# A gated mix of a long convolution and a product-key expert layer on one core: frequency products in whole-array form, folded keys in one burst, skip transforms in pairs, the last tile by halves

## The chip, the cores and the metric

The kernel runs on one core of a Trainium2 chip. The metric is the device time of one execution in microseconds (us), as the median of several runs. The engines are called by their names in the profile: PE is TensorE's matmul, PEld its weight load, DVE is VectorE, ACT is ScalarE, POOL is GpSimd, SP is SyncE, whose queue issues the DMAs.

## What is computed

Two branches read the same 2048 tokens of width 576, and a gate per token mixes them.

```python
g = sigmoid((x * gate_w).sum(-1))
# a: state-space convolution, by FFT of length 4096
K = einsum("dn,dnl,dn->dl", Cc, exp(dt*A*l), dB).real
a = irfft(rfft(pad(u)) * rfft(pad(K)))[:L] + u * Dskip
# b: product-key experts, 32 heads, 64 x 64 keys, 2 experts a head
q = x @ w_q;  s1 = q[:128] @ k1.T;  s2 = q[128:] @ k2.T
top 2 of s1, top 2 of s2, top 2 of their sums -> experts, softmax
b = sum(softmax * gelu(x . u[expert]) * v[expert])
out = g * a + (1 - g) * b
```

## The kernel before

A Python body writes out the whole program in one pass. It keeps a model clock for TensorE (`clock`) and for the other engines (the class `Engine`, lines 108 to 125), and a heap of generators. The main loop issues matmuls of the dense work; after every few of them `pump()` (line 206) lets the generators whose model time has come write their instructions. So the order on every queue is fixed when the program is built, and the chip runs each queue in that order, waiting on semaphores. All matmuls go through `mm` (line 197), hence nearly all rows of the profile have line 204, and all other computing goes through line 124: the tile names tell the work apart.

The dense work is of three kinds. `s` (line 1488) is a score group, one of 128: 14 fp16 matmuls of 512 columns, tokens against the keys that were folded into w_q; its 512 scores a token go through MAX8 and FIND_INDEX8 on DVE (`scores_top`, line 813). `a` (line 1506) is an activation group, one of 128: 14 such matmuls, tokens against the expert table u; ACT or DVE scales the result (`go`) and it is stored to `g_d`. `o` (line 1538) is the output, 16 tiles of 192 fp16 matmuls of 288 columns: 32 weight blocks `wh`, three products each, for two column halves in turn. All `s` and `a` groups come before the first `o`. The last 26 `a` groups are kept for the time after the last `s` group (line 1481).

Beside the dense work run these generators.

- **Folded keys** (`w_half`, lines 465 to 508, and `w_tail`): for each of 8 chunks and 2 halves, w_q times the keys as fp32 matmuls of 64 columns into a 64-column part of the array (tile `wb`), in three bursts of 32, 32 and 16 instructions on the chip; between bursts the generator yields for 2 us, so other matmuls come between. Each burst takes one PSUM bank and one of two `hw` tokens.
- **Convolution kernel** (`k_front`, `k_gen`: tiles `kP`, `kb`; 36 chunks) and the first transforms (`u1_`, `k1_`), with their PSUM banks of the same four as the folded keys in this part of the program.
- **Frequency products** (`products`, lines 1015 to 1105). The 64-point second stage of the transforms, the product and the inverse second stage, in 16 rows by 3 column parts, 48 blocks. A block has 4 fp32 matmuls for the signal (`pu`) and 4 for the kernel (`pk`), each 192 columns into a 64-column part of the array, then a tail on ACT (`us`, `ks`: one copy each from PSUM), two products and two half-size sums on POOL (or DVE), and 4 fp32 matmuls of 192 columns with 64 rows for the inverse (`pv`), issued three blocks later. After the products, the pools of the next stage are opened, `prep(0)` begins, and the last five chunks of the expert table v are split (`v_work(3, 5)`, `v_work(5, 8)`, lines 1136 to 1149).
- **Expert weights** (`prep`, line 1300): one-hot tiles `A`, `Be`, `Bg` on DVE, 128 matmuls `S` a tile in four rounds, products on DVE into `gl`, then the split into `wh`. `o` of a tile needs its `wh`.
- **Skip transform** (`y_part`, lines 1363 to 1399): per tile one load of three tensors, 4 fp32 matmuls (`y`, a 64-column part of the array), two sums on DVE, a scaling on ACT. `finish` (line 1403) adds the output of `o` and stores four row blocks.

The lines of a block's matmuls before (f2 and fi are constants, `half` is the lower or upper 64 partitions):

```python
for r in range(2):
    for z in range(2):
        mm(pb[half[z], PW * r:PW * r + PW], f2[:, 64 * r:64 * r + 64], x[:, z, cs], True, True, 0.17)
...
for r in range(2):
    for z in range(2):
        mm(pv[z][:, :PW], fi[r][half[z]], v[half[z], r], r == 0, r == 1, 0.17)
```

The functions that the diff touches:

Of the kernel before, what the change touches and what calls it, by code (L numbers as in the profile page):

```python
# [24 lines left out]
D = 576  # L25
# [13 lines left out]
FM = 576  # L39
KT = FM + 128  # L40
# [3 lines left out]
def _tables():  # L44
# [43 lines left out]
    cst[:, 256:384] = np.tile(fi[0].reshape(64, 128), (2, 1))  # L88
    cst[:, FM:FM + 128] = np.tile(fi[1].reshape(64, 128), (2, 1))
# [39 lines left out]
def body(ctx: ExitStack, tc: tile.TileContext, xT, au, par, logdt, dskip, gatew, wq, kT, uT, vv,  # L129
# [60 lines left out]
    def dma(o, i):  # L190
# [4 lines left out]
        DQ.dma_start(o, i)  # L195
# [82 lines left out]
    quota(sc=4, wb=0, kb=4, hw=2, slot=9, go=3, m8=2, raw=1, ko=2)  # L278
# [33 lines left out]
    ident, f2, fi = cst[:, 0:128], cst[:, 128:256], (cst[:, 256:384], cst[:, FM:FM + 128])  # L312
# [152 lines left out]
    def w_half(c, h, w):  # L465
        fl = lambda x: x.rearrange("p a b -> p (a b)")
        yield from ready(w)
        acc = newcol(True)
        junk = wj.tile([128, 4, D], BF16, tag="wj", name=f"wj{c}_{h}")
        S.activation(fl(junk), fl(w), AF.Square, accum_out=sc[:, acc])  # L470
        yield from ready(junk)
        while not sk:
            yield 0.3
        tag = side()
        yield from need(tag)
        p = bank(tag, f"wn{c}_{h}")
        mm(p[:, 0:1], onesf, sc[:, acc], True, True, 0.1)
        yield from ready(p)
        s, i = root_scale(p[:, 0:1], kk, True)
        V.tensor_copy(invW[:, 2 * c + h:2 * c + h + 1], i)  # L480
        free(tag, s)
        while c not in halves:
            yield 0.3
        hl, rem, count = halves[c]
        o = slice(256 * h, 256 * h + 256)
        for k in (0, 2, 4):
            yield from need("hw")
            tag = side()
# [12 lines left out]
            yield 2  # L501
        free("slot")
        if c > 0:
            free("raw")
        if h == 0 and c > 0:
            spawn(w_next(c, 1))
        elif h == 1 and c < 7:
            spawn(w_next(c + 1, 0))

    def w_tail(c, k, pb, hl, rem, o, count, s, tag):  # L510
        yield from ready(pb, s)
        if k < 4:
            yield from split(hl[:, 0, k:k + 2, o], hl[:, 1, k:k + 2, o], pb.rearrange("p (k n) -> p k n", k=2), s)
            free(tag, hl)
            free("hw", hl)
# [499 lines left out]
    def products(ff):  # L1015
# [11 lines left out]
        half = [slice(0, 64), slice(64, 128)]  # L1027
        made = []

        def tail(nm, pu, pk, v, vo):  # L1030
            two = lambda x: x[:, 0:2 * PW].rearrange("p (r q) -> p r q", r=2)
            t = lambda g, n: ff.tile([128, 2, PW], F32, tag=g, name=g + nm, bufs=n)
            us, ks, t2 = t("us", 2), t("ks", 2), t("t2", 2)
            bc = lambda r: ks[:, r:r + 1].to_broadcast([128, 2, PW])
# [12 lines left out]
            made.append(nm)  # L1047

        def store(k, hh, vo, pv):
            yield from ready(*pv)  # L1050
            copy2([(vo[:, z, PW * hh:PW * hh + PW], pv[z][:, :PW]) for z in range(2)])
            free("wb", vo)
# [15 lines left out]
        for k in range(16):  # L1068
# [7 lines left out]
            for hh in range(3):  # L1076
# [6 lines left out]
                yield from need("wb", 4 if last else 2)  # L1083
# [12 lines left out]
                spawn(tail(nm, *both, v, vo))  # L1096
                del pb, both
        for last in queue:
# [3 lines left out]
            yield from need("wb", 2)  # L1102
# [260 lines left out]
    def y_part():  # L1363
        def load(t):
            a = oy.tile([128, D], F32, tag="ya", name=f"ya{t}", bufs=3)
            au_load(a, t)
            z = oy.tile([128, 2, D], F32, tag="yz", name=f"yz{t}")
# [6 lines left out]
        nxt = load(0)  # L1374
        for t in range(NT):
            a, z, tf = nxt
            yield from ready(a, z, tf, late=4.0)
            G.tensor_mul(a, a, db)
            while t >= 2 and t - 2 not in finished:
                yield 0.5  # L1380
            yield from need("wb", 2)
            pbs = []
            for hh in range(2):
                pb = bank("wb", f"y{t}_{hh}")
                for pr in range(2):
                    mm(pb[64 * pr:64 * pr + 64, :288], tf[:, pr, :], z[:, pr, 288 * hh:288 * hh + 288], True, True, 0.27)
                pbs.append(pb)
            if t + 1 < NT:
                nxt = load(t + 1)
            yield from ready(a, *pbs)  # L1390
            for hh in range(2):
                ah = a.rearrange("p (j b q) -> p b j q", j=2, b=2)[:, hh]
                V.scalar_tensor_tensor(ah, pbs[hh][:, :288].rearrange("p (j q) -> p j q", j=2), iuk, ah,
                                       op0=OP.mult, op1=OP.add)
                free("wb", a)
            del pbs, pb
            yield from ready(a)
            S.activation(a, a, AF.Copy, scale=gA[:, t:t + 1])
            yt[t] = a

    finished = {}

    def finish(t, po):
# [4 lines left out]
        for hh in range(2):  # L1408
            cs = slice(288 * hh, 288 * hh + 288)
            V.scalar_tensor_tensor(a[:, cs], po[hh][:, :288], om[:, t:t + 1], a[:, cs], op0=OP.mult, op1=OP.add)  # L1410
            free("sc", a)
# [113 lines left out]
    for t in range(NT):  # L1525
# [5 lines left out]
        for b in range(32):  # L1531
            if t == 0 and b % 4 == 0:
                until(lambda: len(vhl) > b // 4)
                wait(ready(vhl[b // 4]))
            vt = vhl[b // 4]
# [4 lines left out]
            pump()  # L1540
        free("slot")
# [44 lines left out]
```

## Time and profile before

| what | value |
|---|---|
| median of 3 runs | 1543.64 us (1543.47 to 1545.33) |
| the profiled execution's own time | 1541.05 us |
| its span | 1539.3 us |
| granted TensorE clock, mean of the span | 0.999 |
| PE busy | 1508.4 us, 98% of the span |
| DVE busy | 1211.6 us, 79% |
| ACT busy | 781.1 us, 51% |
| POOL busy | 543.3 us, 35% |

The profiled execution took 2.6 us less than the median. On the chip every fp32 matmul of the program is two weight loads and two matmul instructions; fp16 matmuls have one of each. A row of the timeline merges consecutive instructions of one kind, so the difference between the starts of two rows is what the first of them cost on its engine. The duration of one matmul contains the way through the array, which the next one overlaps.

### The profile page before, as it was taken

The numbers are of one execution on the slowest core, as the hardware profiler recorded it, in microseconds if no ns is written. First come the engines' busy times: TensorE is split into PE (matmuls) and PEld (weight loads), VectorE is DVE, ScalarE is ACT, GpSimd is POOL, SyncE is SP. The second block draws the span as 40 slices with busy tenths as digits, with TensorE's granted clock in tenths as the row PEclk, the third lists the DMA queues.
The fourth block names the chain that finished last, engine by engine and source line by source line (L and its number), as shares of the span: only waits on it lengthen the run. The fifth ranks groups of instructions, "written<-read, shape, count | busy, mean of one in ns | idle before, by whom it ended". The sixth has DMA issues, their size and how long they took to land.

```text
span 1539.3 us, 37510 instructions
## 1 busy us (share of the span) xinstructions
PE 1508.4 (98%) x14278; PEld 919.0 (60%) x14278; DVE 1211.6 (79%) x4589; ACT 781.1 (51%) x1262; POOL 543.3 (35%) x581
## 2 busy tenths in 40 slices
PE   6999999999999999999999999999999999999998
PEld 4445454445554455656555554445778888788786
DVE  7988998998799957786554579968888788888860
ACT  6548976787859742554444434374432332332320
POOL 0454667646554520136767852240100000000000
PEclk9999999999999999999999999999999999999999
DMA  7344553434444459784755634263553343343310
GB/s 263 91 119 140 162 159 94 138 109 147 139 127 127 128 143 229 243 285 143 231 196 167 208 103 150 90 223 124 152 171 127 104 132 115 115 132 107 122 35 16
DMA packets 153844, 223.41 MB, mean 145 GB/s; under 512 B 11840, under 2 KB 105664, under 8 KB 147008
## 3 DMA queue, kind: packets, MB, share of 16 engines
q1 hardware_dynamic: 153664, 221.02, 46.3%
q8 instruction: 112, 1.84, 0.5%
q14 instruction: 68, 0.56, 0.1%
HBM read 149.67 MB, written 71.30 MB: 144 GB/s over the span
## 4 chain that ended last, share of the span: by engine, by line
PE 84%; DVE 9%; DMA 3%; ACT 2%; issue 1%; SPq 0%; DVEq 0%; ACTq 0%
PE o L204 24%; PE s L204 21%; PE a L204 20%; PE S L204 4%; PE wb L204 3%; PE pv L204 3%; PE pu L204 2%; PE pk L204 2%; DVE i L124 2%; PE kb L204 2%; DVE CS L124 1%; PE y L204 1%; DVE uh L124 1%; DVE m L124 1%; DMA sk_d<-k1o 1%
## 5 line engine op out<-in xcount | busy, mean ns | idle before, releaser
L204 PE MATMUL o<-vhl,wh 128*128 128x288 f16 x3072 | 388.2, 286 | 0.0
L204 PE MATMUL s<-whl,xb 128*128 128x512 f16 x1536 | 367.6, 379 | 1.7 <-DVE xb L124 0.7
L204 PE MATMUL a<-xb,uhl 128*128 128x512 f16 x1536 | 364.5, 379 | 0.0
L204 PEld LDWEIGHTS <-wh 128*128 128x128 f16 x3072 | 295.5, 98 | 79.5 <-issue 7.0
L204 PEld LDWEIGHTS <-xb 128*128 128x128 f16 x1792 | 168.6, 98 | 200.6 <-issue 12.5
L204 PEld LDWEIGHTS <-uhl 128*128 128x128 f16 x1536 | 147.7, 98 | 167.4 <-issue 0.5
L124 DVE FIND_INDEX8 i<-m,s 128x8 uint32<-128x64 f32 x1024 | 206.3, 221 | 0.0
L124 DVE MAX8 m<-s 128x8 f32<-128x64 f32 x1024 | 146.3, 214 | 51.6 <-PE s L204 51.0
L124 ACT ACTIVATE wh<-gl,s_wg 128x1024 f16<-128x1024 f32 x64 | 68.8, 1137 | 179.3 <-DVE gl L124 179.3
L124 POOL TENSOR_TENSOR ya<-ya,db 128x576 f32<-128x576 f32 x16 | 24.7, 1542 | 355.3 <-DMA ya<-in_au_dram 115.7
L124 POOL TENSOR_TENSOR CS<-CS,ex 128x512 f32<-128x512 f32 x72 | 97.8, 1391 | 146.5 <-DVE ex L124 134.8
L124 DVE TENSOR_TENSOR gl<-S,gl 128x256 f32<-128x256 f32 x256 | 90.4, 415 | 20.7 <-PE S L204 18.6
L124 ACT ACTIVATE go<-a,i_a 128x512 f32<-128x512 f32 x86 | 58.8, 686 | 76.7 <-PE a L204 59.7
L124 DVE SCALAR_TENSOR_TENSOR wh<-gl,s_wg,wh 128x1024 f16<-128x1024 f32 x63 | 84.7, 1368 | 13.2 <-ACT wh L124 13.2
L124 ACT ACTIVATE gl<-gl 128x1024 f32<-128x1024 f32 x64 | 63.7, 1046 | 52.6 <-DMA gl<-g_d 52.6
L124 POOL TENSOR_TENSOR e<-aN,rt 128x512 f32<-128x512 f32 x72 | 81.5, 1152 | 25.0 <-PE kb L204 25.0
L124 DVE TENSOR_TENSOR Bg<-Be,vals 128x1024 f16<-128x1024 f16 x128 | 83.9, 696 | 2.2
L124 DVE TENSOR_TENSOR A<-iota_a,vals 128x2048 f16<-128x2048 f16 x64 | 79.3, 1240 | 0.0
L204 PE MATMUL s<-wrem,xb 128*128 128x512 f16 x256 | 76.5, 380 | 1.4 <-DVE xb L124 1.3
L204 PE MATMUL a<-xb,wrem 128*128 128x512 f16 x256 | 76.2, 379 | 0.0
L204 PEld LDWEIGHTS <-A 128*128 128x128 f16 x2048 | 70.6, 97 | 4.6
L204 PE MATMUL S<-Bg,A 128*128 128x64 f16 x2048 | 72.3, 193 | 0.0
(201 smaller groups left out, 2281.5 us busy)
## 6 DMA issues: line engine op xcount, KB each, us to landing
g_d<-go SPq DMA_DIRECT2D x128, 256.0 KB, 2.5
gl<-g_d SPq DMA_DIRECT2D x32, 1024.0 KB, 5.5
wq<-in_wq_dram SPq DMA_DIRECT2D x16, 1152.0 KB, 7.9
us<-in_au_dram SPq DMA_DIRECT2D x64, 144.0 KB, 3.2
su_d<-us SPq DMA_DIRECT2D x32, 288.0 KB, 2.9
sk_d<-k1o SPq DMA_DIRECT2D x32, 288.0 KB, 4.1
vn<-in_vv_dram SPq DMA_DIRECT2D x32, 288.0 KB, 6.0
ui<-su_d SPq DMA_DIRECT2D x16, 576.0 KB, 3.9
```

What stands on the lines that cost most here:

```text
L124: return f(*a, **k)
L204: T.matmul(o, l, r, start=start, stop=stop)
```

## The change

Four edits.

1. **Products in whole-array form.** `pu`, `pk` and `pv` become one fp32 matmul each, 128 rows by 128 columns, 384 moving columns, one PSUM bank each (before: pv took two). The tail on ACT becomes seven copies: `v` (128 partitions), `ux` as two 64-partition copies with the halves exchanged, `kr` and `kx` as two 64-partition copies each, one of them negated. POOL or DVE then does two products, and POOL one sum, all of 384 columns.
2. **Folded keys in one burst.** A half chunk takes three PSUM banks first and then issues all its matmuls without a yield; `hw` has one token instead of two, held until the last part is evacuated.
3. **Skip transform in pairs.** Loads, matmuls and sums go for two tiles at once, with four banks; the `ya` ring has 4 buffers (before 3), `yz` has 2 (before 1).
4. **Last tile by halves.** Tile 15 runs all matmuls of column half 0, then those of half 1; each half is finished and stored by itself, two of the four stores of the last half on ACT's queue.

```diff
-    quota(sc=4, wb=0, kb=4, hw=2, slot=9, go=3, m8=2, raw=1, ko=2)
+    quota(sc=4, wb=0, kb=4, hw=1, slot=9, go=3, m8=2, raw=1, ko=2)
...
+        yield from need("hw")
+        take("hw", "hw")
+        pbs = []
         for k in (0, 2, 4):
-            yield from need("hw")
             tag = side()
             yield from need(tag)
-            take("hw", "hw")
-            pb = bank(tag, f"wb{c}_{h}_{k}")
+            pbs.append((k, tag, bank(tag, f"wb{c}_{h}_{k}")))
+        for k, tag, pb in pbs:
             for j in range(k, min(k + 2, 5)):
...
-            spawn(w_tail(c, k, pb, hl, rem, o, count, s, tag))
-            del pb
-            yield 2
+        for k, tag, pb in pbs:
+            spawn(w_tail(c, k, pb, hl, rem, o, count, s, tag), 0.3 * k)
...
-            S.activation(us, two(pu), AF.Copy)
-            free("wb", us)
+            S.activation(v, two(pu), AF.Copy)
+            S.activation(ux[top], two(pu)[low], AF.Copy)
+            S.activation(ux[low], two(pu)[top], AF.Copy)
+            free("wb", ux)
             yield from ready(pk)
-            S.activation(ks, two(pk), AF.Copy)
-            free("wb", ks)
-            yield from ready(us, ks)
+            S.activation(kr[top], two(pk)[top], AF.Copy)
+            S.activation(kr[low], two(pk)[top], AF.Copy)
+            S.activation(ki[top], two(pk)[low], AF.Copy, scale=-1.0)
+            S.activation(ki[low], two(pk)[low], AF.Copy)
+            free("wb", ki)
+            yield from ready(v, ux, kr, ki)
             M = V if max(V.free, clock[0]) < max(G.free, clock[0]) - 2.5 else G
-            M.tensor_mul(v, us, bc(0))
-            M.tensor_mul(t2, us, bc(1))
-            G.tensor_sub(v[:, 0], v[:, 0], t2[:, 1])
-            G.tensor_add(v[:, 1], v[:, 1], t2[:, 0])
+            M.tensor_mul(v, v, kr)
+            M.tensor_mul(ux, ux, ki)
+            G.tensor_add(v, v, ux)
...
-            pv = [bank("wb", f"pv{z}_{nm}") for z in range(2)]
-            for r in range(2):
-                for z in range(2):
-                    mm(pv[z][:, :PW], fi[r][half[z]], v[half[z], r], r == 0, r == 1, 0.17)
+            pv = bank("wb", f"pv_{nm}")
+            mm(pv[:, 0:2 * PW], fi, v.rearrange("p z q -> p (z q)"), True, True)
...
-                    for r in range(2):
-                        for z in range(2):
-                            mm(pb[half[z], PW * r:PW * r + PW], f2[:, 64 * r:64 * r + 64], x[:, z, cs], True, True, 0.17)
+                    mm(pb[:, 0:2 * PW], f2, x[:, :, cs], True, True)
...
+    def finish_half(t, po, hh):
+        yield from ready(po[hh])
+        a = yt[t]
+        half_rows(t, a, po, hh)
+        yield from ready(a)
+        cs = slice(288 * hh, 288 * hh + 288)
+        for n, (d, o) in enumerate(au_rows(out, t, a)):
+            dma(d[:, cs], o[:, cs], nc.scalar if hh and n % 2 else None)
...
+        if t == NT - 1:
+            until(lambda: t in yt)
+            for hh in range(2):
+                for b in range(32):
+                    for n, (wz, vz) in enumerate(((0, 0), (0, 1), (1, 0))):
+                        mm(po[hh][:, :288], h[wz][:, b, :], vhl[b // 4][:, b % 4, vz, 288 * hh:288 * hh + 288],
+                           b == 0 and n == 0, b == 31 and n == 2)
+                    pump()
+                spawn(finish_half(t, po, hh))
+            break
```

Since the order follows the model clock, it moves as a whole. First, a block of the products on PE, row 5, part 1, with the score group ahead of it. Before (the two `pv` matmuls follow once more):

```order
L204 LDWEIGHTS xb_139
L204 MATMUL s_1_9689<-whl_8265,xb_139 128x512
L204 MATMUL pu_1_9718<-ui_9432,cst 64x192 x4
L204 MATMUL pk_1_9723<-ki_9433,cst 64x192 x4
L204 MATMUL pv_4_1_9728<-vf_1_9557,cst 128x192
L204 MATMUL pv_4_1_9729<-vf_1_9557,cst 128x192
```

And now:

```order
L202 LDWEIGHTS xb_843
L202 MATMUL s_15_10801<-whl_8587,xb_843 128x512
L202 MATMUL pu_1_10812<-ui_10584,cst 128x384
L202 MATMUL pk_1_10814<-ki_10585,cst 128x384
L202 MATMUL pv_1_10816<-vf_1_10675,cst 128x384
L202 LDWEIGHTS xb_843
```

The twelve matmuls became three, and the block now stands beside a later score group.

Second, the folded keys of chunk 2, half 1, on PE. Before, its second burst stood alone between a chunk of the convolution kernel (`kb`) and the next one's phases (`kP`), the other two further off:

```order
L204 MATMUL kb_5054<-Y_4855,CS_4419 32x64 x4
L204 MATMUL kb_5054<-e_4414,CS_4419 32x64 x4
L204 MATMUL wb_1_2_5087<-kt,wq_1_4730 64x64 x16
L204 LDWEIGHTS wb_4125
L204 MATMUL kP_1_5104<-rt,wb_4125 128x512
```

Now the three stand together inside one activation group:

```order
L202 LDWEIGHTS uhl_2576
L202 MATMUL a_0_2_3962<-xb_139,uhl_2576 128x512
L202 MATMUL wb_1_0_3960<-kt,wq_1_3748 64x64 x16
L202 MATMUL wb_1_2_3961<-kt,wq_1_3748 64x64 x16
L202 MATMUL wb_1_4_3971<-kt,wq_1_3748 64x64 x8
```

Three stretches became one, with nothing between them.

Counted over the whole order of PE: folded keys stand in 46 separate stretches before and in 16 now; skip transforms in 16 and 8; `kP` in 50 and 56; the turned indices (`tr`) in 6 and 7. Ahead of the first `k1_` transform stand 2193 matmuls of `s` and `a` groups before and 2400 now. Between the first `pu` and the last `pv` stand 518 of them before and 666 now, and between the last `pv` and the first `o` 677 before and 266 now. On DVE, between the first instruction after the products' pools close (`iota_a`) and the last split of the first tile's weights (`wh0`), there now stand 6 `A`, 6 `Be`, 12 `Bg`, 16 `gl`, 4 `wh`, 11 `vhl` and 4 `go`.

## Rows read from the trace of the kernel before

**Rows 1.** The page: busy time of each engine, and the chain that ended last.

```profile
PE 1508.4 (98%) x14278; PEld 919.0 (60%) x14278; DVE 1211.6 (79%) x4589; ACT 781.1 (51%) x1262; POOL 543.3 (35%) x581
...
PE 84%; DVE 9%; DMA 3%; ACT 2%; issue 1%; SPq 0%; DVEq 0%; ACTq 0%
```

**Rows 2.** Windows: products, then handover; PE, PEld, DVE, ACT, POOL, clock, DMA share, GB/s.

```profile
681.00:925.00 244.00, 244.00 (x2093) 141.56 (x2092) 145.18 (x1038) 111.66 (x282) 173.70 (x237) 1.00 0.54 179
...
985.00:1083.00 98.00, 98.00 (x779) 50.06 (x778) 74.23 (x203) 56.39 (x91) 19.61 (x24) 1.00 0.47 151
```

**Rows 3.** Groups by form on PE: shape, count | busy us, mean ns of one.

```profile
L204 PE MATMUL s<-whl,xb 128*128 128x512 f16 x1536 | 367.6, 379 | 1.7 <-DVE xb L124 0.7 <-DVE whl L124 0.5 <-ACT k1o L124 0.5
...
L204 PE MATMUL pk<-ki,cst 128*64 128x192 f32 x384 | 39.4, 326 | 0.0
```

**Rows 4.** Timeline of PE, 799 to 808 us: start us, us, engine, instruction, count.

```profile
799.59 1.47 PE L204 MATMUL s<-whl,xb 128*128 128x512 f16 x6
800.99 0.69 PE L204 MATMUL wb<-kt,wq 128*64 128x64 f32 x16
801.60 0.61 PE L204 MATMUL s<-wrem,xb 128*128 128x512 f16 x2
802.14 0.87 PE L204 MATMUL pu<-ui,cst 128*64 128x192 f32 x8
...
804.44 2.76 PE L204 MATMUL s<-whl,xb 128*128 128x512 f16 x12
807.04 0.59 PE L204 MATMUL s<-wrem,xb 128*128 128x512 f16 x2
```

**Rows 5.** Timeline of PE, 761 to 763 us: a longer burst of folded keys.

```profile
761.28 1.15 PE L204 MATMUL wb<-kt,wq 128*64 128x64 f32 x32
762.37 0.82 PE L204 MATMUL s<-whl,xb 128*128 128x512 f16 x3
```

**Rows 6.** Timeline of PE and PEld, 624 to 626 us: whole-array fp32 between score matmuls.

```profile
624.67 0.81 PE L204 MATMUL s<-whl,xb 128*128 128x512 f16 x3
...
625.10 0.41 PEld L204 LDWEIGHTS wn<-sc,onesf 128*128 128x128 f32 x2
625.31 0.28 PE L204 MATMUL wn<-sc,onesf 128*128 128x1 f32 x2
...
625.45 0.81 PE L204 MATMUL s<-whl,xb 128*128 128x512 f16 x3
```

**Rows 7.** Timeline of the last microseconds, DVE and SP's queue.

```profile
1534.13 0.94 DVE L124 SCALAR_TENSOR_TENSOR ya<-o,om,ya 128x288 f32<-128x288 f32 x2 [22.65 <-PE o L204]
1535.14 1.73 SPq L195 DMA_DIRECT2D out_dram<-ya  x4
```

**Rows 8.** Timeline of ACT in the products.

```profile
803.12 0.49 ACT L124 ACTIVATE us<-pu 128x384 f32<-128x384 f32 x1 [0.92 <-PE pu L204]
803.71 0.49 ACT L124 ACTIVATE ks<-pk 128x384 f32<-128x384 f32 x1
804.10 0.68 ACT L124 ACTIVATE vj<-vn 128x576 bf16<-128x576 f32 x1
```

**Rows 9.** Groups by form on DVE, 985 to 1083 us.

```profile
L124 DVE TENSOR_TENSOR A<-iota_a,vals 128x2048 f16<-128x2048 f16 x9 | 12.0, 1338 | 0.0
L124 DVE TENSOR_TENSOR gl<-S,gl 128x256 f32<-128x256 f32 x32 | 11.4, 416 | 5.3 <-PE S L204 3.9 <-ACT gl L124 1.3
L124 DVE TENSOR_TENSOR Bg<-Be,vals 128x1024 f16<-128x1024 f16 x16 | 10.3, 688 | 0.3
L124 DVE TENSOR_TENSOR Be<-iota_b,vals 128x1024 f16<-128x1024 f16 x8 | 6.6, 820 | 0.0
...
L124 DVE SCALAR_TENSOR_TENSOR wh<-gl,s_wg,wh 128x1024 f16<-128x1024 f32 x5 | 6.2, 1281 | 0.0
L124 DVE SCALAR_TENSOR_TENSOR vhl<-vhl,sci,vhl 128x576 f16<-128x576 f32 x6 | 5.9, 994 | 1.0 <-ACT vhl L124 1.0
```

**Rows 10.** Waits of SP's DMA queue: for whom, us in total, times, longest.

```profile
SPq L195 <- DMA out_dram<-ya: 50.9, 20, 6.0
```

More of the change, by code (lines that the diff above doesn't have):

```diff
@@ L87, in _tables @@
     cst[:, 128:256] = f2.reshape(128, 128)
[L88 to L89 removed]
+    cst[:, 256:384] = fi.reshape(128, 128)
     cst[:, 384:512] = np.arange(128)[None]
@@ L1026, in products, with tail @@
         parts = {}
[L1027 removed]
+        top, low = slice(0, 64), slice(64, 128)
         made = []
[L1030 to L1034, printed above, removed]
+        def tail(nm, pu, pk, v):
+            t = lambda g: ff.tile([128, 2, PW], F32, tag=g, name=g + nm, bufs=2)
+            ux, kr, ki = t("ux"), t("kr"), t("kx")
+            two = lambda x: x[:, 0:2 * PW].rearrange("p (z q) -> p z q", z=2)
             yield from ready(pu)
[L1036 to L1037 removed]
+            S.activation(v, two(pu), AF.Copy)
+            S.activation(ux[top], two(pu)[low], AF.Copy)
+            S.activation(ux[low], two(pu)[top], AF.Copy)
+            free("wb", ux)
             yield from ready(pk)
[L1039 to L1041 removed]
+            S.activation(kr[top], two(pk)[top], AF.Copy)
[4 more added lines that the diff above has]
+            yield from ready(v, ux, kr, ki)
             M = V if max(V.free, clock[0]) < max(G.free, clock[0]) - 2.5 else G
[L1043 to L1046 removed]
+            M.tensor_mul(v, v, kr)
+            M.tensor_mul(ux, ux, ki)
+            G.tensor_add(v, v, ux)
             made.append(nm)
         def store(k, hh, vo, pv):
[L1050 to L1052 removed]
+            yield from ready(pv)
+            copy(vo[:, :, PW * hh:PW * hh + PW], pv[:, 0:2 * PW].rearrange("p (z q) -> p z q", z=2))
             free("wb", vo)
@@ L1082, in products @@
                     yield from ready(last[3])
-                yield from need("wb", 4 if last else 2)
+                yield from need("wb", 3 if last else 2)
                 nm = f"{k}_{hh}"
@@ L1095, in products @@
                 queue.append((nm, k, hh, v, vo))
-                spawn(tail(nm, *both, v, vo))
+                spawn(tail(nm, *both, v))
                 del pb, both
@@ L1101, in products @@
             yield from ready(last[3])
-            yield from need("wb", 2)
+            yield from need("wb")
             back(*last)
@@ L1373, in y_part @@
         db = row(dskip, "db", oy)
[L1374 to L1378, printed above, removed]
+        nxt = load(0), load(1)
+        for t in range(0, NT, 2):
+            two = nxt
+            yield from ready(*[x for y in two for x in y], late=4.0)
+            for a, z, tf in two:
+                G.tensor_mul(a, a, db)
             while t >= 2 and t - 2 not in finished:
                 yield 0.5
-            yield from need("wb", 2)
+            yield from need("wb", 4)
@@ L1382, in y_part @@
             pbs = []
[L1383 to L1395, printed above, removed]
+            for n, (a, z, tf) in enumerate(two):
+                for hh in range(2):
+                    pb = bank("wb", f"y{t + n}_{hh}")
+                    for pr in range(2):
+                        mm(pb[64 * pr:64 * pr + 64, :288], tf[:, pr, :], z[:, pr, 288 * hh:288 * hh + 288], True, True, 0.27)
+                    pbs.append(pb)
@@ new lines, in y_part @@
+            for n, (a, z, tf) in enumerate(two):
+                yield from ready(a, *pbs[2 * n:2 * n + 2])
+                for hh in range(2):
+                    ah = a.rearrange("p (j b q) -> p b j q", j=2, b=2)[:, hh]
+                    V.scalar_tensor_tensor(ah, pbs[2 * n + hh][:, :288].rearrange("p (j q) -> p j q", j=2), iuk, ah,
+                                           op0=OP.mult, op1=OP.add)
+                    free("wb", a)
+                yield from ready(a)
+                S.activation(a, a, AF.Copy, scale=gA[:, t + n:t + n + 1])
+                yt[t + n] = a
@@ L1396, in y_part, with half_rows @@
             del pbs, pb
-            yield from ready(a)
-            S.activation(a, a, AF.Copy, scale=gA[:, t:t + 1])
-            yt[t] = a
+            if t + 2 < NT:
+                while t and t - 1 not in finished:
+                    yield 0.5
+                nxt = load(t + 2), load(t + 3)
     finished = {}
+    def half_rows(t, a, po, hh):
+        cs = slice(288 * hh, 288 * hh + 288)
+        V.scalar_tensor_tensor(a[:, cs], po[hh][:, :288], om[:, t:t + 1], a[:, cs], op0=OP.mult, op1=OP.add)
+        free("sc", a)
@@ L1403, in finish @@
+    def finish_half(t, po, hh):
+        yield from ready(po[hh])
+        a = yt[t]
+        half_rows(t, a, po, hh)
+        yield from ready(a)
+        cs = slice(288 * hh, 288 * hh + 288)
+        for n, (d, o) in enumerate(au_rows(out, t, a)):
+            dma(d[:, cs], o[:, cs], nc.scalar if hh and n % 2 else None)
+        if hh:
+            finished[t] = 1
     def finish(t, po):
@@ L1540, in body @@
             pump()
+        if t == NT - 1:
+            until(lambda: t in yt)
+            for hh in range(2):
+                for b in range(32):
[4 more added lines that the diff above has]
+                spawn(finish_half(t, po, hh))
+            break
         free("slot")
```

19 lines of the change are left out of this document (8 added, 11 removed).

## The prediction

> **What bounds the kernel now.** I read the page first: PE is busy 98% of the span, and the chain that ended last is PE for 84% [rows 1]. Then the windows of the two stretches that the change works on: in the products, and in the handover after them until the first `o`, PE is busy without a gap, while DVE, ACT and POOL have room (ACT 111.7 of 244 us, DVE 74.2 of 98) [rows 2]. So here a microsecond less on PE is a microsecond less of the whole, as long as nothing new makes PE wait. Last I read PE's timeline start by start, since busy time does not show what a row costs. A score matmul of 512 columns comes every 0.2167 us: twelve take from 804.44 to 807.04 [rows 4].
>
> **What a change of tile shape costs.** Six such matmuls from 799.59 end at 800.89, yet the folded keys begin at 800.99: 0.10 us lost on the way in. The burst of 16 takes 0.61 us, the burst of 32 takes 1.09 [rows 4, 5]: 0.030 an instruction, and 0.13 that does not depend on its length. So every stretch in another tile shape costs 0.23 us beside its work, and a change that merges stretches gains that.
>
> **Products.** The two score matmuls from 801.60 end at 802.03; `pu` begins at 802.14 and the next score at 804.44 [rows 4]: a block takes 2.41 us of PE. What it costs in whole-array form no row shows, so I work it out. A score matmul lasts 379 ns but comes every 217, so 162 ns of a duration is the way through the array; of the 326 ns of a `pk` instruction of 192 columns 164 ns are then its streaming [rows 3]. Two of them stream side by side. A whole-array pass of 384 columns streams 0.327 us; three products of two passes make 1.96 us, with no change of shape from the score matmuls around them. Gain 0.45 us a block, times 48: **21.6 us**. The bounds: nothing better than the loss of all overhead, that is about this value; worse if weight loads show. A whole-array fp32 load takes 0.2 us (two in 0.41), and the nearest row says that it hides: three score matmuls from 624.67 end at 625.32, the load runs below the last of them, and the fp32 matmul starts at 625.31 [rows 6]. If all six loads of a block showed instead, 6 x 0.2 x 48 = 58 us would come on top; I take none of it.
>
> The Trainium skill speaks against that: "TensorE: Matmul & The Clock Gate", Part 3, says that a weight load overlaps with a running matmul only when the two use different row groups. By it whole-array loads would stand bare and the sum would be 58 us worse; the load and matmul just read, both on all 128 rows, contradict it.
>
> **Folded keys.** 46 stretches become 16: 30 x 0.23 = **6.9 us**. **Skip transforms.** 16 become 8: **1.8 us**. The order also splits other work a little more, `kP` by six stretches and `tr` by one: **1.6 us lost**.
>
> **End.** Now two sums of 0.94 us and four store issues of 1.73 us follow the last matmul [rows 7]. Afterwards the first half is finished under the 96 matmuls of the second; what remains is one sum and two issues on each of two queues, side by side: 0.47 + 0.87 = **1.3 us** gained. The wait for the skip transform of tile 15 that now stands ahead of its matmuls costs nothing: it was written out two tiles earlier.
>
> **What the others pay.** ACT: a 384-column copy takes 0.39 us when the next one follows at once (803.71 to 804.10) [rows 8]; five more a block are 94 us. ACT goes from 112 to about 206 us in the products. PE has there 666 dense matmuls (144 us), 48 blocks (94) and some 10 us of keys and turned indices, 248 us: ACT is at 83%, with three blocks, some 15 us, between a tail and its `pv`. POOL loses two half-size sums and gains one of full size, so it stays near its 174 us. One PSUM bank fewer is held in a block.
>
> Keys: a half chunk now holds three of the four banks that the convolution kernel needs too. The order shows what that does: 207 more dense matmuls (45 us) stand ahead of `k1_`, so the convolution comes later against the dense work, but PE has that work to do meanwhile. What it takes is cover at the end: between the last `pv` and the first `o` PE has 266 dense matmuls (58 us) and six `S` stretches of about 1 us, 64 us, where it had 677 (147 us). In them DVE must do, from `iota_a` to the last `wh0`, 6 x 1.34 + 6 x 0.82 + 12 x 0.69 + 16 x 0.42 + 4 x 1.28 + 11 x 0.99, which is 44 us, and four `go` of about the size of a `wh` at half the columns, 3 more [rows 9]: 47 of 64 us. It fits, with 17 us for the loads and the waits between the steps. I take 1 us of new waiting.
>
> Pairs of skip loads put 12 DMA issues on SP's queue at once, 0.43 us each [rows 7], 5 us; behind them stand loads of `gl` and stores, needed a tile (27 us) later. A load into a used `ya` buffer waits for its store, at most 6.0 us now already [rows 10]. I cost this at nothing; the slack of a tile hides it.
>
> **Sum.** 21.6 + 6.9 + 1.8 + 1.3 - 1.6 - 1.0 = 29.0 us, from the profiled execution's 1541.05 to 1512; the median of the runs stands 2.6 higher, so **1514.6 us**.
>
> **Rivals.**
> *Cover too short (faster, by less).* The handover takes longer than its 64 us, because the expert-table chunks, the one-hot tiles and the first split come one after another rather than packed, or ACT's tails make a `pv` wait now and then. For it: DVE has 47 of 64 us and each step waits for a load or another engine. Against it: PE did not wait once in the same stretch before [rows 2]. Some 6 to 15 us of waiting: 1521 to 1530.
>
> *ACT sets the pace of the products (slower).* If the seven copies do not follow each other at once but take their full 0.49 us [rows 8], a block needs 3.4 us of ACT; the rest of ACT's work there, 112 - 48 x 0.39 x 2 = 74 us, is 1.5 a block. 4.9 us against PE's 248 / 48 = 5.2. It decides once ACT needs more than 5.2, and the change loses beyond 5.2 + 29 / 48 = 5.8. At 6.2, with waits of POOL's sums held in ACT's queue in front of other copies, it costs 48 x 1.0 and ends at 1515 + 48 = 1563. Against it: the 0.39 us, and ACT's queue seldom stood behind anything else than PE.
>
> *Loads in the open (slower).* As priced above, 1515 + 58 = 1573; against it the row of the whole-array fp32 matmul. The Trainium skill's rule named above is this case.
>
> *Nothing merged.* The order shows that the stretches did merge, so I give this no chance.
>
> **How the numbers follow.** Forecast 0.68 (1508 to 1521), short cover 0.20 (1521 to 1532), ACT 0.06, loads 0.04, the gains and losses just cancelling 0.02. The range leaves out the two slower cases, the tie and some of each edge: 1507 to 1530. A difference of 0.2%, 3 us, is about what a measurement of this kernel tells from none: faster 0.88, same 0.02, slower 0.10.
>
> **What would show it.** Right: three rows of one product a block, each starting 0.65 us after the one before, and a score matmul 1.96 us after `pu`; 16 bursts of keys of 80 instructions in about 2.5 us; PE busy in the products with ACT at 80 to 85%; no gap ahead of the first `o`; 1.3 us less from the last matmul to the end. Wrong: PE idle ahead of `pv` with ACT or POOL as releaser, PE idle between the last `a` and the first `o` with `wh` or `vhl` as releaser, or blocks of the products above 2.2 us.

## The result, and the profile after

The changed kernel takes 1520.9 us (median of four runs, 1518.4 to 1523.3) against 1544.5 beside it: a ratio of 0.9846, 95% interval 0.9828 to 0.9865. It is faster, by 23.6 us of the 29.0 forecast, at the upper edge of what the forecast called its own case. The profiled execution took 1521.13 us, its span 1519.4 (1539.3 before). Each profile shows a single execution, so the difference of the two spans, 19.9 us, is not that of the medians.

The page of the changed kernel, busy time of each engine, to be held against [rows 1]:

```profile
PE 1484.3 (98%) x13410; PEld 899.0 (59%) x13414; DVE 1227.3 (81%) x4583; ACT 884.0 (58%) x1456; POOL 533.0 (35%) x528
```

PE is 24.1 us less busy, ACT 103 us more. But the span fell by only 19.9 us: PE's idle time, span less busy time, grew from 30.9 to 35.1 us. So the question is where new idle time stands. Three windows of the changed kernel: the products, from the first `pu` to the last `pv`; the handover to the first `o`; the output to the last `o` (columns as in [rows 2]):

```profile
744.00:1000.00 256.00, 251.22 (x1255) 129.39 (x1253) 162.61 (x969) 233.65 (x515) 181.37 (x209) 1.00 0.56 186
1000.20:1063.20 63.00, 63.00 (x458) 31.71 (x457) 51.97 (x71) 39.59 (x54) 10.32 (x6) 1.00 0.75 250
1063.20:1515.50 452.30, 450.70 (x5057) 364.52 (x5055) 370.87 (x593) 131.38 (x133) 29.41 (x16) 1.00 0.35 112
```

The handover is full, as forecast. In the products PE, without a gap before, is idle for 4.8 us, and ACT is busy for 234 of 256 us, 91%. The five longest waits of PE in that window (who waits for whom, us in total, times, longest):

```profile
PE s L202 <- ACT ux L122: 1.5, 4, 0.6
PE tr L202 <- ACT kx L122: 0.9, 1, 0.9
PE tr L202 <- ACT vals L122: 0.7, 1, 0.7
PE pv L202 <- DVE i L122: 0.7, 1, 0.7
PE pk L202 <- ACT kx L122: 0.6, 1, 0.6
```

Four of the five name ACT. PE's timeline of the change, one burst of keys, and then a block with the score groups around it:

```profile
311.41 2.55 PE L202 MATMUL wb<-kt,wq 128*64 128x64 f32 x80
...
799.80 0.59 PE L202 MATMUL s<-wrem,xb 128*128 128x512 f16 x2
800.24 0.81 PE L202 MATMUL pu<-ui,cst 128*128 128x384 f32 x2
800.88 0.81 PE L202 MATMUL pk<-ki,cst 128*128 128x384 f32 x2
801.52 0.81 PE L202 MATMUL pv<-vf,cst 128*128 128x384 f32 x2
802.17 2.75 PE L202 MATMUL s<-whl,xb 128*128 128x512 f16 x12
```

The three products start 0.64 us apart, and the block takes 800.24 to 802.17, 1.93 us, with nothing lost on the way in. Each of their six weight loads runs below the matmul pass ahead of it; those of `pk`, 0.19 us each, start with the second pass of `pu` and with the first of `pk`:

```profile
800.56 0.51 PEld L202 LDWEIGHTS pk<-ki,cst 128*128 128x128 f32 x2
```

The burst, one of the 14 of chunks 1 to 7, has all 80 matmuls in one stretch.

Two losses were in no part of the prediction. The first is at the start: the first `a` group starts at 41.13 us, 4.6 us later than before (36.52). PE's timeline of the first `a` group, before (L204) and after (L202):

```profile
36.52 2.75 PE L204 MATMUL a<-xb,uhl 128*128 128x512 f16 x12
...
41.13 2.11 PE L202 MATMUL a<-xb,uhl 128*128 128x512 f16 x9
```

PE's timeline of the start after the change:

```profile
17.34 2.55 PE L202 MATMUL wb<-kt,wq 128*64 128x64 f32 x80
...
23.02 0.38 PE L202 MATMUL s<-whl,xb 128*128 128x512 f16 x1 [0.80 <-ACT whl L122]
25.91 4.80 PE L202 MATMUL s<-whl,xb 128*128 128x512 f16 x11 [2.52 <-DVE whl L122]
30.55 0.60 PE L202 MATMUL s<-wrem,xb 128*128 128x512 f16 x2
```

Windows of the same stretch (columns as in [rows 2], the clock third from the end):

```profile
20.00:25.00 5.00, 1.14 (x5) 0.71 (x6) 2.46 (x8) 5.00 (x10) 0.00 (x0) 0.87 0.20 73
25.00:30.00 5.00, 4.09 (x10) 1.43 (x10) 4.94 (x9) 5.00 (x8) 0.00 (x0) 0.50 0.01 2
```

The keys are done at 19.9, yet the second score matmul waits for `whl` until 25.9. And then eleven matmuls take 4.64 us from start to start (25.91 to 30.55) where twelve take 2.6 [rows 4]: PE had stood still most of the time since 20 us, and the granted clock is 0.50, the lower of the two levels (1.2 GHz). ACT shows why `whl` is late:

```profile
19.17 1.91 ACT L122 ACTIVATE uhl<-us 128x2048 bf16<-128x2048 f32 x1 [1.40 <-DMA us<-in_uT_dram]
20.98 0.19 ACT L122 ACTIVATION_READ_ACCUMULATOR uhl<-us 128x1 f32 x1
21.08 0.61 ACT L122 ACTIVATE uhl<-ur 128x512 bf16<-128x512 f32 x1
21.60 0.19 ACT L122 ACTIVATION_READ_ACCUMULATOR uhl<-ur 128x1 f32 x1
21.69 0.71 ACT L122 ACTIVATE xb<-xs,sci 128x512 f16<-128x512 f32 x1
22.30 1.24 ACT L122 ACTIVATE whl<-wb,sci 128x512 f16<-128x512 f32 x2
```

Since the burst is written out whole before its evacuations, these stand on ACT's queue behind the squares of the expert table (`uhl`), which wait for their load.

The second loss is PE's longest single wait after the first `a` group, and again slow matmuls behind it:

```profile
270.42 5.30 PE L202 MATMUL a<-xb,uhl 128*128 128x512 f16 x12 [3.08 <-DVE i L122]
275.52 0.99 PE L202 MATMUL a<-xb,wrem 128*128 128x512 f16 x2
```

The window of the first 5 us of these matmuls:

```profile
270.00:275.00 5.00, 4.58 (x11) 1.64 (x12) 4.94 (x8) 0.00 (x0) 3.14 (x3) 0.50 0.39 125
```

From 260 to 270 us DVE is busy for 9.9 of 10 us, at first with a chunk of the convolution kernel; the search through the scores comes after that, and an `a` group waits for it. The granted clock is 0.50 again, and the fourteen matmuls take 5.9 us (270.42 to 276.34) where 3.0 is usual [rows 4]: 2.9 us on top of the wait of 3.1. The kernel before has a wait of 2.2 us in this part (254 us) and a clock of 0.66 in the 5 us after it. The wait of 3.1 us is in every version here that has the keys of chunks 1 to 7 in one burst, and in none that has them in three; no version repairs it.

### The profile page after: what moved, and what is told of

It reads as the page before. It is cut to its first block, busy times and chain, and to the rows that moved or that the text cites. A ratio compares the mean times of both kernels' runs of the same rounds, so it can differ in the third digit from the quotient of the medians.

```text
span 1519.4 us, 35924 instructions
## 1 busy us (share of the span) xinstructions
PE 1484.3 (98%) x13410; PEld 899.0 (59%) x13414; DVE 1227.3 (81%) x4583; ACT 884.0 (58%) x1456; POOL 533.0 (35%) x528
## 5 line engine op out<-in xcount | busy, mean ns | idle before, releaser
L202 PE MATMUL o<-vhl,wh 128*128 128x288 f16 x3072 | 387.3, 286 | 0.0
L202 PE MATMUL s<-whl,xb 128*128 128x512 f16 x1536 | 369.4, 381 | 6.1 <-DVE whl L122 2.5
L202 PE MATMUL a<-xb,uhl 128*128 128x512 f16 x1536 | 365.4, 381 | 3.1 <-DVE i L122 3.1
L202 PEld LDWEIGHTS <-wh 128*128 128x128 f16 x3072 | 295.9, 98 | 76.2 <-issue 3.5
L202 PEld LDWEIGHTS <-xb 128*128 128x128 f16 x1792 | 173.3, 98 | 209.2 <-issue 15.7
L202 PEld LDWEIGHTS <-uhl 128*128 128x128 f16 x1536 | 148.9, 99 | 177.6 <-issue 6.0
L122 POOL TENSOR_TENSOR ya<-ya,db 128x576 f32<-128x576 f32 x16 | 29.4, 1838 | 338.2 <-DVE Bg L122 195.5
L122 DVE SCALAR_TENSOR_TENSOR wh<-gl,s_wg,wh 128x1024 f16<-128x1024 f32 x64 | 87.9, 1405 | 11.3 <-ACT wh L122 11.3
L122 DVE TENSOR_TENSOR A<-iota_a,vals 128x2048 f16<-128x2048 f16 x64 | 84.4, 1319 | 0.0
L202 PE MATMUL s<-wrem,xb 128*128 128x512 f16 x256 | 76.2, 379 | 0.4 <-DVE xb L122 0.4
L202 PE MATMUL a<-xb,wrem 128*128 128x512 f16 x256 | 76.6, 381 | 0.0
L202 PEld LDWEIGHTS <-A 128*128 128x128 f16 x2048 | 70.7, 97 | 6.5 <-issue 1.2
L202 PE MATMUL S<-Bg,A 128*128 128x64 f16 x2048 | 73.0, 193 | 1.6 <-DVE Bg L122 1.5
```

What stands on the lines that cost most here:

```text
L122: return f(*a, **k)
L202: T.matmul(o, l, r, start=start, stop=stop)
```

## Experiments

Two theories are tried here: the missing microseconds lie (1) at the start, by the burst of chunk 0, and (2) in the products, by ACT's seven copies. The rival to both is that the two are accidents of a new order, made up or lost elsewhere anyway. The medians and ratios of all versions:

| version | us | ratio to before, 95% interval |
|---|---|---|
| the change | 1520.89 | 0.9846 (0.9828 to 0.9865) |
| start_old | 1517.35 | 0.9831 (0.9817 to 0.9844) |
| keys_old | 1522.85 | 0.9860 (0.9845 to 0.9876) |
| products_only | 1524.43 | 0.9870 (0.9855 to 0.9885) |
| act_order | 1522.23 | 0.9855 (0.9839 to 0.9872) |
| ux_dve | 1515.51 | 0.9825 (0.9809 to 0.9841) |
| act_extra | 1538.29 | 0.9966 (0.9952 to 0.9979) |
| skip_end_old | 1520.46 | 0.9853 (0.9838 to 0.9868) |
| ux_dve_start | 1513.89 | 0.9810 (0.9797 to 0.9824) |
| order_start | 1529.85 | 0.9911 (0.9898 to 0.9925) |
| ux_start_model | 1532.16 | 0.9928 (0.9914 to 0.9941) |
| keys_old_ux_model | 1520.99 | 0.9853 (0.9837 to 0.9868) |
| ux_start_low | 1512.50 | 0.9803 (0.9789 to 0.9817) |

### The start

```diff
         for k in (0, 2, 4):
...
+            if c == 0:
+                keys(w, h, c, *pbs[-1])
+                spawn(w_tail(c, k, pbs[-1][2], hl, rem, o, count, s, tag))
+                yield 2
```

> Only the keys of chunk 0 go back to three bursts, each with its own tail at once; all else is the changed kernel. Theory (the one burst of chunk 0 puts the evacuations of the keys behind the squares of the expert table on ACT, so the first score groups come late and then run at a lower granted clock): the first a group starts near 36.5 us again instead of 41.1, and the time falls by 3.5 to 5 us, to about 1516 to 1517.5. Rival (the late start is made up later, because ACT and DVE then have less of a backlog, or it comes from the loads and not from the keys): the first a group stays near 41 us, or the time stays within 2 us of 1520.9.

Measured: 1517.35 us, 3.5 less (2.3 by the ratios; their intervals overlap), and PE's timeline has the start back:

```profile
22.28 1.69 PE L202 MATMUL s<-whl,xb 128*128 128x512 f16 x7
24.23 1.24 PE L202 MATMUL s<-whl,xb 128*128 128x512 f16 x5 [0.27 <-DVE whl L122]
...
37.20 2.75 PE L202 MATMUL a<-xb,uhl 128*128 128x512 f16 x12
```

The granted clock is 1.00 there. The 3.9 us at the first `a` are still there at the end of the span (4.8 us shorter): the late start was not made up later.

### The keys and the products, one without the other

keys_old takes the whole second edit back; products_only is the kernel before with the first edit alone.

```diff
 keys_old
-    quota(sc=4, wb=0, kb=4, hw=1, slot=9, go=3, m8=2, raw=1, ko=2)
+    quota(sc=4, wb=0, kb=4, hw=2, slot=9, go=3, m8=2, raw=1, ko=2)
...
+            spawn(w_tail(c, k, pb, hl, rem, o, count, s, tag))
+            del pb
+            yield 2
 products_only
+            mm(pv[:, 0:2 * PW], fi, v.rearrange("p z q -> p (z q)"), True, True)
...
+                    mm(pb[:, 0:2 * PW], f2, x[:, :, cs], True, True)
```

> The changed kernel with its second edit undone: all keys in three bursts, two hw tokens. Theory: one burst gains 30 stretches x 0.23 = 6.9 us in the middle and loses 4.6 at the start, so undoing it costs about 2.3 us: 1522 to 1525, with the first a group near 36.5 us and 46 or so stretches of keys. Rival A (the term of the prediction holds whole and the late start has another cause): 1527 to 1529. Rival B (one burst is worth less than 0.23 a stretch, because the matmuls lose the same at every change of shape whether bursts are long or short): below 1520, the edit was a loss.

Measured: 1522.85 us. Undoing the edit costs 2.0 us, as expected, though the intervals overlap. With start_old beside it the parts come out: 5.5 us (4.5 by the ratios, 7.3 between the two profiled spans) for 28 stretches merged in the middle (46 to 18), where 28 x 0.23 = 6.4 were forecast, less the loss at the start.

> The kernel before with the first edit alone. Theory: a block falls from 2.41 to about 1.94 us, 48 x 0.47 = 22.6, and ACT, at 91% in the products, gives back some 4 to 5 us of PE waiting: 17 to 19 us below the kernel before, about 1526 to 1528, with PE idle in the products and 0.50 us for each copy on ACT. Rival (the PE waiting in the products comes from the changed order of the other three edits, not from the tails): 22 to 23 us below, 1521 to 1523, PE busy in the products without a gap.

Measured: 1524.43 us, 19.9 below the kernel before. The theory's 17 to 19 us assumed 4 to 5 us of waiting; PE was idle in the products for 1.7 us only, so neither side was met. Alone, the products stand beside 627 dense matmuls in 248 us, and ACT is busy for 93% of that time, no less than in the change (91%):

```profile
683.40:931.00 247.60, 245.89 (x1329) 128.93 (x1328) 174.70 (x1205) 229.78 (x499) 177.32 (x200) 1.00 0.58 196
```

So a high share of ACT does not by itself say how long PE waits, 1.7 us here and 4.8 in the change; what differs between the two is the other three edits and the order that comes of them.

### ACT's copies

Three edits of the tail: the copies in another order (which also waits for `pk` before the first copy), `ux` on DVE, one copy made twice.

```diff
 act_order
-            yield from ready(pu)
+            yield from ready(pu, pk)
             S.activation(v, two(pu), AF.Copy)
-            S.activation(ux[top], two(pu)[low], AF.Copy)
-            S.activation(ux[low], two(pu)[top], AF.Copy)
-            free("wb", ux)
-            yield from ready(pk)
             S.activation(kr[top], two(pk)[top], AF.Copy)
             S.activation(kr[low], two(pk)[top], AF.Copy)
+            S.activation(ux[low], two(pu)[top], AF.Copy)
+            S.activation(ux[top], two(pu)[low], AF.Copy)
+            free("wb", ux)
             S.activation(ki[top], two(pk)[low], AF.Copy, scale=-1.0)
             S.activation(ki[low], two(pk)[low], AF.Copy)
 ux_dve
-            S.activation(ux[top], two(pu)[low], AF.Copy)
-            S.activation(ux[low], two(pu)[top], AF.Copy)
+            V.tensor_copy(ux[top], two(pu)[low])
+            V.tensor_copy(ux[low], two(pu)[top])
 act_extra
             S.activation(kr[top], two(pk)[top], AF.Copy)
+            S.activation(kr[top], two(pk)[top], AF.Copy)
```

> The changed kernel with the seven copies of a tail in another order, so that two pairs have the same source half and the same target half (kr low then ux low, ux top then kx top); nothing else. Theory (a copy starts under the end of the one before only if both use the same partitions): these two pairs come 0.37 to 0.39 us apart and the other pairs 0.50; ACT is 48 x 2 x 0.11 = 10.6 us less busy and the PE idle time in the products falls by 1 to 3 us. Rival (any copy of 64 partitions runs alone): all pairs stay at 0.50 us and the time stays within 2 us.

A tail on ACT in the changed kernel, in ACT's timeline:

```profile
860.09 0.48 ACT L122 ACTIVATE vf<-pu 128x384 f32<-128x384 f32 x1
860.58 0.98 ACT L122 ACTIVATE ux<-pu 64x384 f32<-64x384 f32 x2
861.59 0.98 ACT L122 ACTIVATE kr<-pk 64x384 f32<-64x384 f32 x2
862.59 0.98 ACT L122 ACTIVATE kx<-pk 64x384 f32<-64x384 f32 x2
```

The same in act_order:

```profile
862.86 0.98 ACT L122 ACTIVATE kr<-pk 64x384 f32<-64x384 f32 x2 [0.15 <-PE pk L202]
863.74 0.97 ACT L122 ACTIVATE ux<-pu 64x384 f32<-64x384 f32 x2
864.61 0.97 ACT L122 ACTIVATE kx<-pk 64x384 f32<-64x384 f32 x2
```

In the change every copy takes its full 0.50 us. Reordered, the pairs begin 0.88 and 0.87 us apart: one step of 0.48 to 0.50, and one of 0.39, where a copy has the source half and the target half of the one before. The half of the theory on ACT's copies held, and ACT fell by 14 us in the products; PE's idle time there went from 4.8 to 0.2 us. But the time did not fall: it is 1522.23 us, within 2 us of the change as the rival had it, since idle time came back after the first `o`. Its windows of handover and output:

```profile
1003.00:1056.40 53.40, 53.40 (x413) 27.30 (x412) 43.18 (x58) 34.22 (x46) 11.28 (x8) 1.00 0.79 275
1056.40:1516.50 460.10, 452.24 (x5063) 364.82 (x5060) 377.46 (x602) 138.03 (x142) 34.22 (x20) 1.00 0.35 110
```

The handover is 53 us instead of 63, and PE then waits for 7.9 us in the output (1.6 in the change), 7.4 of them for `Bg`.

> The changed kernel with the two exchanged copies of the signal (ux) on DVE in place of ACT. Theory (ACT, at 91% in the products, is what PE waits for there): ACT loses 48 x 2 x 0.50 = 48 us in the products and stands at about 74%, DVE gains some 46 us and stands at about 80%; PE's idle time between the first pu and the last pv falls from 4.8 us to below 1.5, and the time by 3 to 5 us, to 1516 to 1518, unless the handover gives it back as it did with the reordered copies (then 1519 to 1522, with PE idle after the first o). Rival (the waits come from the scores on DVE, whose index search is the releaser in some of them): PE idle stays or grows, and the time does not fall.

Measured: 1515.51 us, 5.4 less by the medians (3.2 by the ratios; their intervals overlap a little). Its window of the products:

```profile
743.00:995.00 252.00, 250.31 (x1264) 130.72 (x1262) 213.76 (x1056) 189.79 (x426) 185.83 (x212) 1.00 0.56 189
```

ACT is at 75%, DVE at 85%, PE idle for 1.7 us, and no wait of PE there is put down to ACT any more. Idle time and time both just miss the theory's figures (below 1.5 us; 1516 to 1518), but its reading holds; the rival, by which the idle time stays or grows, falls.

> The changed kernel with one of the seven copies of a tail (kr top) made twice: 48 x 0.50 = 24 us more of ACT in the products, nothing else added. Theory (ACT near the pace of the products): ACT would need 258 us where PE has 251, so PE's idle time in the products grows from 4.8 to 10 to 20 us, and the time by about as much, to 1526 to 1536. Rival (the waits are single accidents of the order, ACT has slack to spare): PE idle stays near 5 us and the time within 3 us of 1520.9.

Measured: 1538.29 us, 17.4 more and above the theory's range. PE's idle time in its products is 12.1 us, within it:

```profile
741.00:1008.00 267.00, 254.93 (x1253) 128.79 (x1252) 166.16 (x985) 249.96 (x548) 177.84 (x206) 0.99 0.52 178
```

The output after it waits for 5.7 us as well, 4.8 of them for `Bg`. So 24 us of ACT cost 17, of which the trace shows 7.3 as new idle time in the products and 4.1 in the output: ACT has little slack left in the change.

This run also limits the theory of act_order. The doubled copy of `kr` has equal halves on both sides, and yet came 0.50 to 0.52 us after the first:

```profile
860.43 1.50 ACT L122 ACTIVATE kr<-pk 64x384 f32<-64x384 f32 x3
```

So equal halves alone do not make a step of 0.39. Every such step between these copies also went on to another target tile and another source bank; which of the two is needed was not tried.

### Skip transforms and the last tile

skip_end_old takes edits 3 and 4 back; of edit 3 the main lines are

```diff
-        for t in range(0, NT, 2):
...
+        for t in range(NT):
...
-            yield from need("wb", 4)
+            yield from need("wb", 2)
```

> The changed kernel with edits 3 and 4 undone: skip transforms one tile at a time, the last tile like the others. The two do not touch each other and are read apart in the trace. Theory: the time from the start of the last o to the end grows from 3.9 to 5.4 us (1.5, forecast 1.3); 8 more stretches of the skip transforms cost 8 x 0.16 to 0.23, 1.3 to 1.8 us; together 2.8 to 3.3 us, 1523.5 to 1524.5. Rival (the output stage is bound by something else than PE's rows there, or the pairs of loads hold up others by as much as they gain): less than 1.5 us, and the loads of pairs would show as waits of PE in the output stage of the changed kernel that are gone here.

Measured: 1520.46 us, no difference. Its start happened to be 1.4 us earlier, so the trace is read from the first `o` (1061.95) to the end of its span (1519.3): 457.4 us, against 1063.20 to 1519.4, 456.2, in the change. The two edits gain 1.2 us of the 3.1 forecast. The end is as forecast: in the change, the last sum and stores are

```profile
1515.79 0.52 DVE L122 SCALAR_TENSOR_TENSOR ya<-o,om,ya 128x288 f32<-128x288 f32 x1 [11.24 <-PE o L202]
1516.33 0.78 SPq L193 DMA_DIRECT2D out_dram<-ya  x2
1516.38 0.85 ACTq L193 DMA_DIRECT2D out_dram<-ya  x2
```

in place of two sums of 0.94 us together and four issues of 1.73 together [rows 7]: from the start of the last `o` to the end of the span 3.9 us, 5.4 in skip_end_old. In return, PE waits in the output stage of the change for `Bg` four times, and not once in skip_end_old:

```profile
PE S L202 <- DVE Bg L122: 1.5, 4, 0.6
```

So the theory holds for the rows, and the rival for the time: what edit 3 gains is given back.

### Both repairs, and a model with another cost of the copies

ux_dve_start joins start_old and ux_dve. order_start and ux_start_model also raise the planner's cost of a 64-partition copy, ux_start_low lowers it:

```diff
         t = 0.085 + 0.00083 * size(out)
+        if out.shape[0] == 64 and size(out) == 384:
+            t += 0.11
```

> The changed kernel with both repairs that each won alone: chunk 0's keys in three bursts, and the ux copies on DVE. Theory (the two losses lie in different places and add): 1520.9 less 3.5 for the start and less 4 to 5.4 for ACT, 1511 to 1514, first a group near 37 us, PE idle in the products below 1.5 us. Rival (they hit the same later wait, so the second is worth nothing): 1515 to 1517.5.

Measured: 1513.89 us, 7.0 below the change (5.6 by the ratios, where the two repairs alone gave 2.3 and 3.2; 3.5 and 5.4 by the medians): the two repairs add, within the noise. PE is idle for 1.7 us in the products.

> The changed kernel with chunk 0's keys in three bursts, the reordered copies of a tail, and the model's cost of a 64-partition copy raised by 0.08 us, nearer to the 0.45 to 0.50 that they take. Theory (the reordered copies lost their gain because the model, too short on ACT, put the handover's steps too late): PE idle in the products stays below 1 us and the wait for Bg after the first o falls below 3 us from 7.4: 1511 to 1514. Rival (the wait for Bg comes from DVE's own work in the handover, which the cost of ACT does not touch): Bg wait stays near 7 us, 1516 to 1519.

> Both repairs of the start and of ux, and the model's cost of a 64-partition copy raised by 0.11 us. Theory (after ux is on DVE, ACT has room enough and the model's cost of its copies decides nothing): within 2 us of the version with the two repairs, 1511 to 1514. Rival (a truer cost also packs the handover better): below 1510.5, with less PE waiting after the last pv.

Measured: 1529.85 and 1532.16 us. PE does not wait in the products of order_start, as its theory said, but both times miss every range: ux_start_model, which differs from ux_dve_start by the cost alone, is 18.3 us slower, although the new cost is nearer to the truth. PE's waits from the last `pv` to the end in ux_start_model:

```profile
PE S L204 <- DVE Bg L122: 13.1, 6, 6.3
PE o L204 <- DVE wh L122: 2.2, 1, 2.2
```

The order suggests why. With dearer copies the planner puts the blocks further apart and fills in with dense matmuls, and those are then missing in the handover, where they cover DVE's work on the first tiles. Dense matmuls left for the handover, and PE's idle time in the output stage (first to last `o`):

| version | dense matmuls in the handover | PE idle in the output, us |
|---|---|---|
| before | 677 | 0.8 |
| the change | 266 | 1.6 |
| ux_dve_start | 257 | 2.0 |
| act_extra | 271 | 5.7 |
| act_order | 221 | 7.9 |
| ux_start_model | 168 | 15.3 |
| order_start | 142 | 12.6 (and 2.7 in the handover) |

The count is not all of it: act_extra, with ACT late, waits for 5.7 us at 271. The theory that the missing cover does the harm was then tried with the same dear copies where the stock of dense work is large, all keys in three bursts:

> The version with ux on DVE and the raised model cost, but with all keys in three bursts, so that dense work is used up later: by the order, 442 dense matmuls stand between the last pv and the first o, where the version with one burst has 168. Theory (the raised model cost did harm only because it drew dense matmuls out of the handover into the products): no PE idle time worth telling after the last pv, and about 5 us below the kernel with the keys alone undone (1522.9), 1516 to 1520. Rival (the raised cost harms by itself, whatever stands in the handover): 1530 or more, with PE waiting for Bg or wh again.

Measured: 1520.99 us; PE waits for 0.8 us after the last `pv`. The time is 1.0 above the range (there was less waiting to win: 2.9 us of idle time in the products of keys_old), but the rival's 1530 is far off. So the raised cost does not do its harm of 18 us by itself; it takes the short handover. A small harm of its own is not excluded, since the same kernel without the raised cost was not run.

> Both repairs (chunk 0's keys in three bursts, ux on DVE), with the model's cost of a 64-partition copy lowered by 0.15 us: by the order 310 dense matmuls and 7 rounds of S in the handover, where the version with the model's own cost has 257 and 6. Theory (257 stand just at the edge of what the handover needs, so more cover gains little): PE's wait for Bg falls from 1.8 us to below 1, while PE may wait 1 to 3 us more in the products, whose blocks now stand closer than POOL and ACT finish them: 1511 to 1516. Rival (the handover still costs several us): below 1510.

Measured: 1512.50 us, the lowest of the study, 0.9803 of the time before (0.9789 to 0.9817); from 1513.89 it cannot be told apart. PE's wait for `Bg` did not fall (2.3 us after 1.8), and PE waited for 0.4 us only in the products, so both halves of that expectation missed; the time fits the theory that more cover gains little here.

## Why the prediction was right, and what it missed

**Products, 21.6 us: right.** 2.41 - 1.93 = 0.48 us a block, 23.0 us; the edit alone gave 19.9 with 1.7 us of idle time in the products. The loads hide, so the rival *Loads in the open* falls: the three products of a block start 0.64 us apart, the streaming of two passes, with two weight loads each (0.2 us apiece [rows 6]) below them on the same 128 rows. The rule of the Trainium skill ("TensorE: Matmul & The Clock Gate", Part 3) that loads overlap only across different row groups does not hold in this trace.

**Folded keys, 6.9 us: the rate about right, the place not.** 5.5 us for 28 stretches, 0.20 each where 0.23 was forecast. The failed step is "PE has that work to do meanwhile": true of most of what stands behind chunks 1 to 7, but behind the keys of chunk 0 stands the first score group and nothing else that is ready. That costs 4.6 us in the profile, 2.3 of it by the granted clock of 0.50 after the wait (4.64 us for eleven matmuls of 0.217); repairing it gave 3.5 us. The wait at 267 us, which all versions with one burst share, is a second place where it does not hold.

**ACT, 83%: the failed price.** The 0.39 us of [rows 8] belongs to a copy followed by one with the same start on both sides, into another tile and from another bank. The seven copies of a tail change the source half or the target half at every step and took 0.50, so ACT stood at 91%. The sum's 1.0 us of new waiting stood for the handover; for the products it had none, and PE waited there for 4.8 us. The rival *ACT sets the pace* had the right 3.4 us a block, and its 4.9 in all (233.65 / 48 = 4.87), but not its 1563: against PE's 5.2 that was close enough to wait at times, not to lose. The time landed on the border between the forecast and *Cover too short*, which had named ACT's tails as one of its causes.

**Handover: right as built, and at the edge.** 63.0 us, full, with DVE busy for 52 of them (47 reckoned). The rival's mechanism is real: act_order, ux_start_model and order_start, whose products take 712 to 791 dense matmuls in place of 666, left 221 to 142 for the handover and paid there, and act_extra paid with 271.

**Skip transforms 1.8 and end 1.3: 1.2 of 3.1.** The end came as reckoned (1.5); the pairs' gain came back as the wait for `Bg`. Whether "the slack of a tile hides it" failed for the loads, or something else in a pair holds DVE up, was not tried.

By terms, with the forecast's 6.9 and -1.6 for what was not measured whole: 23.0 + 6.9 - 1.6 + 1.2 - 4.6 - 4.8 = 20.1 us, against 19.9 between the two profiled spans. That it closes so well is partly luck. The keys measured less than 6.9, and the sum leaves out the second loss, at 267 us, and what the kernel before loses near there. PE's idle time from the first `a` to the first `pu` is 12.4 us before, 9.8 in the change and 15.6 in products_only, which has the order of the kernel before up to there: single executions differ by 3 us in this stretch.

Without the misses at the start and on ACT the kernel runs in 1513.9 us, where 1514.6 was forecast. This is partly luck too: the products gave 1.4 us more than the forecast, edits 3 and 4 gave 1.9 less, the second loss is still in, and with `ux` on DVE it is no longer the kernel that was forecast.

## What to carry to other kernels

Price an added instruction by a row with the same neighbour, not only the same size: half-array copies on ACT cost 0.50 or 0.39 us by what stood next to them. When merging steps is argued to be free because other work covers it, look at the first instance apart, where no other work is ready yet, and at what the engines that feed that work are doing meanwhile. And where an order is planned by a model, a stage's spare work is a stock: count what every edit leaves of it for the next stage, since a truer cost in one place can spend it.

## What the runs showed of the hardware

- A copy on ACT of 384 fp32 columns from PSUM lasts 0.48 to 0.49 us. The next one came 0.39 us after it where source and target started at the same partitions (act_order, `kr` to `ux` and `ux` to `kx`, 48 times each), and 0.48 to 0.51 us after it where source or target changed half (the change, the three steps of a tail to another tile). With equal halves but the same tile written again it came 0.50 to 0.52 us later (act_extra), so equal halves were not enough.
- A whole-array fp32 matmul of 384 columns comes every 0.64 us in the blocks of the change, both its weight loads hidden.
- After PE had waited for `whl` at the start, the granted clock was 0.50 and eleven score matmuls took 4.64 us; in start_old, without that wait, it was 1.00. After the wait of 3.1 us at 267 us it was 0.50 again, and fourteen matmuls took 5.9 us in place of 3.0.
